# Moving the split, the store and the next load of a converted chunk within its eight steps

## The chip, the cores and the metric

The kernel runs on one core of one Trainium2 chip. The metric is the device time of one execution in microseconds (us). Three runs of the kernel before gave a median of 2088.47 us, from 2087.82 to 2095.43 us. In the listings PE is TensorE, DVE VectorE, ACT ScalarE, POOL GpSimd, and SP the engine that issues most of the DMAs, in order, one after another.

## The reference

Three parts follow one another. The first is attention with random features, and its output is reshaped to 2304 tokens of 512 values. The second is a mixture of eight experts in which every token goes through every expert. The third is one more pair of matrices, which are given in doubles (float64).

```python
x = np.ascontiguousarray(attn_out.transpose(0, 2, 1, 3)).reshape(B * S, H * D)
for e in range(E):                       # E = 8, w1[e]: 512 x 1024, w2[e]: 1024 x 512
    h = np.maximum(x @ w1[e], 0.0)
    ye = h @ w2[e]
    out += P[:, e:e + 1] * ye
h = x @ w_in                             # 512 x 2048, float64
g = h - np.tanh(h)
return (g @ w_out).astype(np.float32)    # 2048 x 512, float64
```

P is a gate that is normalized over rows and columns eight times.

## The kernel before

**Tiling.** The 2304 tokens are cut into three superblocks of 768 tokens. After the attention the program goes through the superblocks for the experts (kind 0, s = 0, 1, 2), then through the superblocks for the last pair of matrices (kind 1). In kind 0 a superblock is a loop over 32 groups Q (8 experts, 4 quarters of the hidden width each). Each float32 operand is held as a high and a low part (float32r), and a product is three matmuls: high by high, high by low, low by high. The first layer of a group in superblocks 1 and 2 is `quad7` (seven products of a Strassen scheme, in PSUM banks a, b and e, line 1259), and between its products stands the second layer, `group` (line 1434). A steady group holds 84 matmuls of 384 columns.

**Order.** The order on every engine is the order in which the program emits its instructions. Each engine works through its own queue in order and waits on semaphores. Between two products the program calls `between`, which among other things calls `tick` twice. So a group has 14 ticks. A tick advances the weight preparation `wprep` (in superblock 2: one load of a prepared unit `u`, line 296, and one of a prepared unit `y`, line 318, both on SP), the preparation of x, and in 26 of 32 ticks the background generator `bg`. Once every four groups `load_p` (line 1524) loads the gate values of the next expert, spread over all partitions, also on SP.

**The conversion.** In the third superblock the background generator is `convert(..., fine=True)`. It turns the last matrices' doubles into float32, one chunk of 128 x 256 doubles after another. One chunk takes eight steps of the generator. Its instructions are, on DVE: a clamp of the high words (line 1199), a shift (1203), a merge (1206), an exponent mask (1210), a product with the low words (1213); then an absolute value on ACT (1216) and an addition on POOL (1217); then a last product on DVE (1222), which gives the chunk `x` in float32. Of the 64 chunks, 27 are converted in the first superblock and 37 in the third: 32 whose result is split at once, and 5 "plain" ones whose float32 result is stored as it is (line 1226).

**The split chunks.** For these, `split_up` makes the high part (`V.tensor_copy`, line 1179) and the low part (`low`, line 1172), both written over the raw tile `r` from which the doubles were read. `put` (line 1176) stores `r` to DRAM, in one DMA or two, 48 in all, and `ld` (line 1186) loads the doubles of a later chunk. There are three raw tiles `r`: three loads are made ahead, and the load of chunk n+3 goes into the tile of chunk n. So SP holds that load until the store of chunk n has left the tile. The list `after` holds what is still to be done for the chunk just converted; `step()` takes one entry from it at each of the generator's yields, so its first entry is taken in the first step of the next chunk. Before the change the list of a split chunk has eight entries: nothing, nothing, high part, nothing, low part, nothing, store, load. For a plain chunk it is the load alone.

Of the kernel before, what the change touches and what calls it, by code (L numbers as in the profile page):

```python
# [20 lines left out]
def performer_moe_kernel(ctx, tc, q, k, v, omega, wg, w1, w2, win64, wout64, out):  # L21
# [1135 lines left out]
    def convert(raws, work, fine):  # L1157
        V = nc.vector
        bits = lambda w: struct.unpack("f", struct.pack("I", w))[0]
        big, small = bits(0x47EFFFFF), bits(0x38100000)  # L1160
        after = []

        def step():
            f = after.pop(0) if after else None
            if f:
                f()

        def split_up(x, r, dst, key):
            both = r.rearrange("p n t -> p (n t)").rearrange("p (h n) -> p h n", h=2).bitcast(F32R)

            def low():
                V.tensor_tensor(both[:, 1], x, both[:, 0].bitcast(F32), ALU.subtract)

            def put():
                for to, src in dst(both.bitcast(F32)):
                    nc.sync.dma_start(to, src)
                left[key] -= 1

            return [None, None, lambda: V.tensor_copy(both[:, 0], x), None, low, None, put]

        def ld():
            if not cjobs or halt[0]:
                return None
            key, src, dst = cjobs.pop(0)
            r = raws(f"r64_{len(cjobs)}")
            nc.sync.dma_start(r, src.bitcast(U32).rearrange("p (n t) -> p n t", t=2))
            return r, dst, key

        nx = [ld(), ld(), ld()] if fine else [ld()]
        for _ in range(16 if fine else 1):  # L1190
            yield
        while nx[0]:
            r, dst, key = nx.pop(0)
            if not fine:
                nx.append(ld())
            lo, hi = r[:, :, 0], r[:, :, 1]
            c, t, h, x = work(f"cw{converted[0]}")
            cf, xf = c.bitcast(F32), x.bitcast(F32)
            V.tensor_scalar(cf, hi.bitcast(F32), big, -big, ALU.min, ALU.max)
            if fine:  # L1200
                yield
                step()
            V.tensor_scalar(t, c, 3, 0x3FFFFFFF, ALU.logical_shift_left, ALU.bitwise_and)
            yield
            step()
            V.scalar_tensor_tensor(h, c, 0xC0000000, t, ALU.bitwise_and, ALU.bitwise_or)
            if fine:
                yield
                step()
            V.tensor_scalar(t, h, 0xFF800000, None, ALU.bitwise_and)  # L1210
            yield
            step()
            V.scalar_tensor_tensor(xf, lo, 2.0**-52, t.bitcast(F32), ALU.mult, ALU.mult)
            yield
            step()
            nc.scalar.activation(cf, cf, AF.Abs)
            nc.gpsimd.tensor_tensor(xf, xf, h.bitcast(F32), ALU.add)
            yield
            step()
            yield  # L1220
            step()
            V.scalar_tensor_tensor(xf, cf, small, xf, ALU.is_ge, ALU.mult)
            if callable(dst):
                after.extend(split_up(xf, r, dst, key))
            else:
                nc.sync.dma_start(dst, xf)
                left[key] -= 1
            if fine:
                after.append(lambda: nx.append(ld()))
            converted[0] += 1  # L1230
            yield
            step()
        while after:
            step()
            yield
# [459 lines left out]
    for st in stages:  # L1695
        kind, s = st
        if kind == 0 and s == 0:
            for Q in range(NQ):
# [4 lines left out]
                if Q == 2 * NQE + 3:  # L1703
                    phase.close()
                    pace[1] = 3
                    cv = phase.enter_context(tc.tile_pool(name="cvp", bufs=1))
                    bg.append(
                        convert(
                            lambda n: cv.tile([P, CW, 2], U32, tag="r64", name=n, bufs=2),
                            lambda n: [  # L1710
                                cv.tile([P, CW], U32, tag=f"c{i}", name=f"{n}{i}", bufs=1 + i // 3) for i in range(4)
                            ],
                            False,
                        )
                    )
                    next(bg[0])
# [26 lines left out]
        elif kind == 0:  # L1743
            for Q in range(NQ):
# [6 lines left out]
                if s == 2 and Q == 1:  # L1751
                    halt[0] = False
                    cjobs[:] = later_jobs + cjobs
                    pace[4] = 26
                    bg.append(
                        convert(
                            lambda n: rawp.tile([P, CW, 2], U32, tag="rs", name=n, bufs=3),
                            lambda n: [
                                x[:, i] for x in [sump.tile([P, 4, CW], U32, tag="s", name=n)] for i in range(3)
                            ] + [cxp[0].tile([P, CW], U32, tag="x", name=f"{n}x")],  # L1760
                            True,
                        )
                    )
# [103 lines left out]
```

## Time and profile before

| | |
|---|---|
| median of 3 runs | 2088.47 us |
| the profiled execution's own time | 2088.66 us |
| its span (first to last instruction) | 2086.9 us |
| PE busy | 2021.9 us (97%) |
| DVE busy | 1574.3 us (75%) |
| ACT, POOL busy | 1395.7, 1410.0 us |
| DMA, mean over the span | 241 GB/s |

The span is counted from the first instruction; between its end and the own time lie 1.8 us. In a listing of windows each row is one stretch: its ends and its length in us, then for each engine the busy time and the number of instructions, then TensorE's granted clock as a share of full speed, the busy share of the DMA engines, and GB/s. In a listing of waits the three numbers are the sum in us, the number of times, and the longest. In a listing of one line the durations are in ns (least, median, greatest), followed by the first and the last start in us. In a timeline a row is the start, the duration, engine, line, operation, output<-input, count, and in brackets how long the engine had been idle and what ended that.

### The profile page before, as it was taken

Reading aid. Unit: us, or ns where it says so; the run is one execution under the profiler, and the core shown is the slowest. Engines: PE = TensorE matmul, PEld = TensorE weight load, DVE = VectorE, ACT = ScalarE, POOL = GpSimd, SP = SyncE. Lnnn points to the kernel's source line nnn. Section 1 sums busy time; section 2 is a strip of 40 time slices with the busy share of each in tenths; the row PEclk is TensorE's granted clock in tenths of the full one; section 3 lists DMA queues with packets and bytes.
Section 4 is the critical chain, followed back from the end, with each engine's and each line's share of the span. In section 5 each row is a group of like instructions: output and inputs, shape, how many; then the busy total and the mean of one; then the engine's idle time right before and its main releaser. Section 6 shows DMA issues by size and latency. Waiting matters only on the chain.

```text
span 2086.9 us, 37530 instructions
## 1 busy us (share of the span) xinstructions
PE 2021.9 (97%) x11408; PEld 1885.1 (90%) x11408; DVE 1574.3 (75%) x3056; ACT 1395.7 (67%) x3426; POOL 1410.0 (68%) x1783
## 2 busy tenths in 40 slices
PE   9999999999999999999999999899999999999999
PEld 7777989899998999999999998888999988999998
DVE  8885867989886565766656677577876489999897
ACT  7884343344443577778777687677777778777775
POOL 7876877878874588888888666566666555254352
PEclk9999999999999999999999999999999999999999
DMA  6545977897876688999988877787888661441410
GB/s 171 137 134 181 369 276 261 288 336 269 282 265 230 211 312 289 330 344 357 320 299 310 326 270 271 269 312 255 263 296 306 232 217 54 139 152 65 168 46 31
DMA packets 357081, 503.24 MB, mean 241 GB/s; under 512 B 72448, under 2 KB 169616, under 8 KB 356880
## 3 DMA queue, kind: packets, MB, share of 16 engines
q1 hardware_dynamic: 350736, 493.44, 69.2%
q10 hardware_dynamic: 6144, 7.40, 1.1%
q8 instruction: 92, 1.51, 0.3%
q14 instruction: 109, 0.89, 0.1%
HBM read 351.75 MB, written 148.97 MB: 240 GB/s over the span
## 4 chain that ended last, share of the span: by engine, by line
PE 69%; DMA 10%; DVE 9%; POOL 5%; issue 3%; ACT 2%; SPq 1%; ACTq 0%; DVEq 0%; POOLq 0%
PE l L1575 20%; PE Y L1434 13%; PE b L1259 11%; PE p L1535 8%; PE e L1259 7%; PE a L1259 7%; DMA st<-r 3%; PE X L1434 2%; DMA u<-st 2%; POOL tmp L633 2%; DMA y<-st 1%; POOL eq L793 1%; DMA r<-in_moe_w_out_dram 1%; DMA r<-in_moe_w_in_dram 1%; DMA st<-y 1%
## 5 line engine op out<-in xcount | busy, mean ns | idle before, releaser
L1434 PE MATMUL Y<-h,y 128*128 128x384 f32 x2394 | 491.5, 338 | 14.1 <-ACT Y L1426 13.6
L1575 PE MATMUL l<-v,h 128*128 128x512 f32 x2016 | 482.6, 392 | 5.3 <-ACT x L113 1.8
L1575 PEld LDWEIGHTS l<-v,h 128*128 128x128 f32 x2016 | 375.4, 188 | 83.2 <-ACT h L1563 3.5
L1434 PEld LDWEIGHTS Y<-h,y 128*128 128x128 f32 x2394 | 424.0, 190 | 22.3 <-ACT Y L1426 21.2
L1259 PE MATMUL b<-x,u 128*128 128x384 f32 x1728 | 351.4, 338 | 20.4 <-DVE t L1358 13.4
L1343 POOL TENSOR_TENSOR h<-t,h 128x384 fp32r<-128x384 f32 x223 | 230.4, 1033 | 192.6 <-ACT h L1340 166.9
L1450 ACT COPY seven<-Y 128x384 f32<-128x384 f32 x534 | 247.4, 481 | 145.0 <-PE Y L1434 142.0
L1259 PEld LDWEIGHTS b<-x,u 128*128 128x128 f32 x1728 | 306.2, 189 | 28.3 <-DVE t L1358 15.1
L1426 ACT COPY Y<-seven 128x384 f32<-128x384 f32 x558 | 262.8, 488 | 4.0 <-DVE seven L1448 4.0
L1343 POOL TENSOR_TENSOR h<-h,h 128x384 fp32r<-128x384 f32 x192 | 202.7, 1060 | 51.6 <-ACT h L1340 43.2
L1259 PE MATMUL a<-x,u 128*128 128x384 f32 x1152 | 231.8, 335 | 1.8 <-POOL u L116 1.3
L1259 PE MATMUL e<-x,u 128*128 128x384 f32 x1152 | 232.3, 336 | 0.0
L1564 POOL TENSOR_TENSOR h<-t,h 128x384 fp32r<-128x384 f32 x94 | 95.9, 1020 | 187.9 <-ACT h L1563 185.7
L1535 PE MATMUL p<-x,u 128*128 128x384 f32 x1152 | 210.1, 337 | 2.3 <-DMA u<-st 1.6
L1535 PEld LDWEIGHTS p<-x,u 128*128 128x128 f32 x1152 | 202.6, 188 | 6.7 <-DMA u<-st 2.2
L1259 PEld LDWEIGHTS a<-x,u 128*128 128x128 f32 x1152 | 202.7, 188 | 3.5 <-POOL u L116 1.7
L1259 PEld LDWEIGHTS e<-x,u 128*128 128x128 f32 x1152 | 203.8, 189 | 0.0
L116 POOL TENSOR_TENSOR v<-rs,v 128x256 fp32r<-128x256 f32 x152 | 121.3, 827 | 53.6 <-ACT v L113 41.1
L1340 ACT CAST h<-t 128x384 fp32r<-128x384 f32 x224 | 115.7, 517 | 50.7 <-DVE t L1336 28.6
L1610 DVE SCALAR_TENSOR_TENSOR acc<-l,pt,acc 128x512 f32<-128x512 f32 x144 | 104.8, 744 | 27.8 <-PE l L1575 26.1
L113 ACT CAST u<-s 128x256 fp32r<-128x256 f32 x128 | 49.4, 409 | 105.9 <-POOL u L116 42.2
L116 POOL TENSOR_TENSOR u<-s,u 128x256 fp32r<-128x256 f32 x128 | 97.4, 778 | 22.5 <-ACT u L113 21.8
(410 smaller groups left out, 3711.8 us busy)
## 6 DMA issues: line engine op xcount, KB each, us to landing
u<-st SPq DMA_DIRECT2D x496, 256.0 KB, 5.2
y<-st SPq DMA_DIRECT2D x336, 256.0 KB, 5.0
st<-u SPq DMA_DIRECT2D x224, 256.0 KB, 3.8
rs<-in_moe_w_dram SPq DMA_DIRECT2D x128, 256.0 KB, 4.7
st<-y SPq DMA_DIRECT2D x128, 256.0 KB, 5.7
st<-v SPq DMA_DIRECT2D x96, 256.0 KB, 5.2
rq<-in_moe_w_dram SPq DMA_DIRECT2D x32, 512.0 KB, 4.8
v<-st SPq DMA_DIRECT2D x24, 512.0 KB, 6.0
```

What stands on the lines that cost most here:

```text
L113: nc.scalar.copy(dst[:, 0], src)
L116: eng.tensor_tensor(dst[:, 1, i : i + w], src[:, i : i + w], dst[:, 0, i : i + w].bitcast(F32), ALU.subtract)
L1259: nc.tensor.matmul(ps[:, :TB], u[:, wi, c], x[:, xi, c], start=(start and m == 0), stop=(stop and m == 5), skip_group_check=True,)
L1340: nc.scalar.copy(H[k][:, 0], src)
L1343: eng.tensor_tensor(H[k][:, 1], src, H[k][:, 0].bitcast(F32), ALU.subtract)
L1426: nc.scalar.copy(cell[0], xacc[i][:, d])
L1434: nc.tensor.matmul(ps, uw[i, g][0][:, wi, d * P : (d + 1) * P], Hs[g][i][:, hi], start=(n == 0 and not cell), stop=(n == 3 * len(gs) - 1), ...
L1450: nc.scalar.copy(xacc[i][:, d], ps)
L1535: nc.tensor.matmul(ps, u1[f + i][:, wi, c], ux[state["x0"] + 2 * t + i][:, xi, c], start=(m == 0), stop=(m == 11))
L1564: nc.gpsimd.tensor_tensor(lo, s, hi.bitcast(F32), ALU.subtract)
L1575: nc.tensor.matmul(ps, hh[f][0][:, hi, t : t + P], u2[n + f][:, wi], start=(f == 0 and i == 0), stop=(f == len(hh) - 1 and i == 2),)
L1610: V.scalar_tensor_tensor(a, ps, p[:, e : e + 1], a, ALU.mult, ALU.add)
```

## The change

A split chunk's list becomes: high part, low part, nothing, store, nothing, nothing, nothing, load. So the high part is made in the first step behind the conversion, the low part in the second, the store is issued in the fourth, and the load stays in the eighth. For a plain chunk in the third superblock seven empty entries are put ahead of its load, so that it too comes in the eighth step.

```diff
@@ in split_up
-            return [None, None, lambda: V.tensor_copy(both[:, 0], x), None, low, None, put]
+            return [lambda: V.tensor_copy(both[:, 0], x), low, None, put, None, None, None]
@@ behind a chunk's conversion
             else:
                 nc.sync.dma_start(dst, xf)
                 left[key] -= 1
+                after.extend([None] * 7 if fine else [])
             if fine:
                 after.append(lambda: nx.append(ld()))
```

## Rows read from the trace of the kernel before

**Rows 1.** Windows: superblock 1 (30 groups), then superblock 2 (29 groups).
```profile
709.80:1149.28 439.48, 437.79 (x2522) 436.64 (x2521) 279.04 (x490) 342.52 (x844) 367.92 (x420) 1.00 0.91 317
1181.03:1647.41 466.38, 436.74 (x2437) 428.13 (x2437) 323.20 (x607) 350.02 (x847) 298.30 (x299) 0.98 0.81 277
```

**Rows 2.** Windows: two of seven long groups, a steady one, sum of eight.
```profile
1256.32:1274.91 18.59, 16.41 (x85) 16.09 (x85) 13.73 (x26) 12.94 (x33) 10.14 (x11) 0.91 0.82 288
1306.34:1329.66 23.32, 17.31 (x85) 16.67 (x85) 11.41 (x25) 12.58 (x30) 11.39 (x12) 0.85 0.78 279
...
1409.64:1424.20 14.56, 14.56 (x86) 14.56 (x85) 11.23 (x25) 11.27 (x29) 10.10 (x12) 1.00 0.84 284
sum 150.35, PE 126.77 PEld 122.94 DVE 95.13 ACT 96.59 POOL 84.76; mean PE 15.85 PEld 15.37 DVE 11.89 ACT 12.07 POOL 10.59
```

**Rows 3.** Waits of PE, DVE and SP in 1181.03:1647.41.
```profile
PE b L1259 <- DVE t L1358: 13.4, 5, 5.3
...
DVE cw L1199 <- DMA r<-in_moe_w_out_dram: 39.6, 11, 10.1
...
DVE cw L1199 <- DMA r<-in_moe_w_in_dram: 21.8, 9, 5.8
...
SPq L1186 <- DMA st<-r: 125.3, 32, 6.4
SPq L318 <- PE Y L1434: 35.5, 29, 6.5
```

**Rows 4.** Timeline 1308:1324: one late load and whom it holds.
```profile
1312.18 0.59 SPq L1176 DMA_DIRECT2D st<-r  x1
...
1318.39 0.34 SPq L1186 DMA_DIRECT2D r<-in_moe_w_out_dram  x1
...
1321.51 0.29 DVE L1199 TENSOR_SCALAR cw<-r 128x256 f32<-128x256 f32 x1 [10.14 <-DMA r<-in_moe_w_out_dram]
...
1323.19 1.33 PE L1259 MATMUL b<-x,u 128*128 128x384 f32 x3 [5.27 <-DVE t L1358]
```

**Rows 5.** Line 1176, the store of the split parts, in superblock 2.
```profile
L1176 SPq DMA_DIRECT2D st<-r x48: 370/525/1328, 1209.2 to 1574.2; - x48
...
DMA to landing us min/median/max: 4.3/5.5/7.5
```

**Rows 6.** Landing times of line 1186 (doubles), then of line 1524 (gate), superblock 2.
```profile
DMA to landing us min/median/max: 2.5/3.1/6.6
...
DMA to landing us min/median/max: 8.6/9.1/9.8
```

**Rows 7.** Lines 296 and 318 (loads of units), then 1199 (clamp), superblock 2.
```profile
L296 SPq DMA_DIRECT2D u<-st x202: 319/430/2703, 1180.4 to 1640.1; - x101
...
L318 SPq DMA_DIRECT2D y<-st x202: 319/385/1287, 1181.4 to 1647.1; - x101
...
L1199 DVE TENSOR_SCALAR cw<-r x37: 281/487/1109, 1191.2 to 1603.3; 128x256 f32<-128x256 f32 x37
```

**Rows 8.** Timelines: gate load beside its group's first product, superblock 1, then 2.
```profile
753.48 1.20 PE L1259 MATMUL a<-x,u 128*128 128x384 f32 x6
753.52 0.43 SPq L1524 DMA_DIRECT2D pb<-pd  x1
...
1290.62 1.20 PE L1259 MATMUL a<-x,u 128*128 128x384 f32 x6
...
1299.54 0.49 SPq L1524 DMA_DIRECT2D pb<-pd  x1
```

**Rows 9.** Lines 1179 (high part) and 1172 (low part): a short and a long.
```profile
L1179 DVE CAST r<-cw35x x1: 285/285/285, 1293.5 to 1293.5; 128x256 fp32r<-128x256 f32 x1
...
L1179 DVE CAST r<-cw40x x1: 1110/1110/1110, 1358.6 to 1358.6; 128x256 fp32r<-128x256 f32 x1
...
L1172 DVE TENSOR_TENSOR r<-cw34x,r x1: 1234/1234/1234, 1285.9 to 1285.9; 128x256 fp32r<-128x256 f32 x1
L1172 DVE TENSOR_TENSOR r<-cw35x,r x1: 416/416/416, 1295.2 to 1295.2; 128x256 fp32r<-128x256 f32 x1
```

## The prediction

> **What bounds the kernel now.** I read the windows first, one group of the loop at a time. TensorE sets the end nearly everywhere: in superblock 1 the 30 groups take 439.48 us [rows 1], and a steady group takes 14.56 us [rows 2], so 30 x 14.56 = 436.8 and only 2.7 us are lost. Superblock 2, the one that converts, takes 466.38 us for 29 groups [rows 1], and 29 x 14.56 = 422.2: 44.1 us are lost there. The reader should see that the number of matmuls per group is the same and only the time differs. The loss is not even: seven groups and a steady one take 150.35 us together [rows 2], so the seven take 135.8 where 7 x 14.56 = 101.9 would do, 33.9 of the 44.1. The other 22 groups lose 10.2, or 0.47 each. In the longest groups the granted clock is below 1 as well (0.85 and 0.91 [rows 2]): TensorE ran partly at 1.2 in place of 2.4 GHz behind its own pauses, which is part of the loss and goes with them.
>
> Then the waits, engine by engine, backwards. The greatest wait of TensorE is for a DVE addition of the group's scheme (13.4 us in 5 [rows 3]). The greatest waits of DVE are those of the clamp, which opens a chunk, for its doubles: 39.6 + 21.8 = 61.4 us in 20 [rows 3]. The greatest of SP, by far, is that of the doubles' load for the store of the split parts out of the same raw tile: 125.3 us in 32, 3.9 each [rows 3]. One place shows the chain whole [rows 4]: the store is issued at 1312.18, the load only at 1318.39, the clamp starts at 1321.51 after 10.14 us of idle DVE, and TensorE, which needs the DVE instructions queued behind the clamp, has then idled for 5.27 us.
>
> The doubles should not be late: their load is emitted nine steps ahead of the clamp that reads them. It is SP that is behind. The gate load, which SP gets to in the same order, starts 0.04 us after its group's first product in superblock 1 and 8.92 us after it in superblock 2 [rows 8].
>
> **The change part by part.** Steps first. A chunk takes 8 steps; with 26 of 32 ticks and 14 ticks in 14.56 us a step is 1.28 us where nothing is lost (a chunk 10.24 us). Measured with the losses: 37 clamps from 1191.2 to 1603.3 [rows 7], 11.4 us a chunk, 1.43 a step.
>
> *Store from the seventh step to the fourth.* The store lands 5.5 us after its issue (4.3 to 7.5 [rows 5]). Before, the load follows one step later: 5.5 - 1.4 = 4.1 us of stall, against 3.9 measured. After, four steps lie between, 4 x 1.28 = 5.1 us: a stall of 0.4 at the median and 2.4 at the longest landing. Over 32 chunks this is 13 to 77 us in place of 125.3; I take 15, since the median is what repeats.
>
> When SP is behind, the steps' time doesn't count, only what it has to issue. A chunk's 9.85 ticks hold as many unit loads, of 0.41 us each (median 0.430 and 0.385 [rows 7]): 4.0 us. Its 1.5 stores of 0.53 [rows 5] add 0.8, its load 0.34 [rows 4]: 5.2 us. Before, 1.2 unit loads (0.5 us) lie between store and load, the stall is 5.5 - 0.5 = 5.0, the sum 10.2 of 10.24 us: once SP is late, it stays late, and every gate load, which lands 3.6 us later than a store (9.1 against 5.5 [rows 5, 6]), throws it back further. After, 4.9 unit loads (2.0 us) lie between, the stall is 3.5, the sum 8.7: SP makes up 1.5 us with each chunk, of which the gate loads, one in four groups or 5.7 chunks, take 0.6. So it catches up, slowly.
>
> What that gives the doubles: from the load's place to its clamp are 9 x 1.28 = 11.5 us; landing takes 3.1 (at most 6.6 [rows 6]), so SP may be 8.4 us late (4.9 in the bad case). It is 8.92 late now. Without the 3.5 us a chunk of avoided stall it stays inside that.
>
> *The loss that goes.* I charge the seven long groups to the late doubles. From one side: the seven fall to what the other 22 lose, 29 x 0.47 = 13.6 remain, 30.5 are gained. From the other: the 22 also owe half of theirs to late doubles, 5 more, 35.6. DVE's additional instructions stay, and with them the small collisions. I take 33.5, between the two.
>
> *High and low part two and three steps earlier.* Same instructions, no new wait: both read what DVE itself has written, and the raw tile's doubles are already used up. The store stays two steps behind the low part. Queued behind them on DVE are the next chunk's clamp and shift and the group's additions. A high part takes 0.29 or 1.11 us, a low part 0.42 or 1.23 [rows 9]; if all of them were long where all are short now, DVE has 32 x (0.82 + 0.81) = 52 us more; if the reverse, as much less. I take nothing, since both places lie between instructions of the same kind, and keep the bound for a rival.
>
> *Plain chunks.* Five of them; two further loads of doubles move seven steps back and then have the slack of every other chunk, 11.5 us. The seven empty steps at the end, 9 us, lie in the superblock's last groups, past the last clamp at 1603.3 [rows 7], while the superblock goes on beyond 1647 [rows 1]. Nothing waits for them: 0, and if the cover were gone, still no instruction in them.
>
> *What is late next.* SP's waits for TensorE to give up unit tiles (35.5 us in 29 [rows 3]) are SP being ahead, and grow. DVE's collisions stay and are in the 10 to 13.6 us.
>
> Sum, against the profiled execution's own 2088.66 us (span 2086.9 and 1.8 around it; the median of the runs is 2088.47, 0.2 less): 2088.7 - 33.5 = 2055.2, so 2055.
>
> **Two rules of the Trainium skill beside it.** The store's landing is 5.5 us for 256 KB [rows 5]. The Trainium skill, "DMA: Bandwidth & Descriptors", section "Anatomy of one DMA — SWDGE (gpsimd) path", gives about 2.0 us plus bytes over 436 GB/s, an estimate of 2.6 us by that page (its path is GpSimd's). By it SP's sum before would be 5.2 + 2.1 = 7.3 of 10.24 us, SP would not be behind at all and the change would be worth nothing; the trace disagrees, with 3.9 us of stall.
>
> High parts come in two lengths, 0.29 and 1.11 us [rows 9]. The Trainium skill, "SBUF — State Buffer", section "Who interferes with whom", has a DVE copy and a GpSimd instruction shut each other out of a shared port pair, whoever issues first. By it the first step is a poor place for the copy, since GpSimd has just been busy for the same chunk; the two lengths agree with the rule, and what it could cost is the third rival.
>
> **The rivals.** *Half of it.* SP stays behind for long stretches, since gate loads and waits for unit tiles throw it back faster than 0.9 us a chunk makes up; the stall then is 3.5 in place of 3.9 or 5.0, and about half of the late doubles stay. For it: at least one of the longest groups, 1306.34, comes straight after a gate load [rows 2, 8]. Against it: superblock 1 has the same gate loads and no lag [rows 8]. Time: 2088.7 - 17 = 2072.
>
> *Nothing.* The doubles are late for the gate loads alone and the store's wait is only where SP happens to stand. Against it: 125.3 us of SP's 466 in that wait. Time 2088.
>
> *Slower: the crowd at the chunk's end.* The last product, the high part, the clamp, the low part and the shift now come one behind the other on DVE, and the group's additions queue behind them. DVE's lost time costs TensorE at 44.1 / 61.4 = 0.72. To use up 33.5 us DVE must lose 46.6, or 1.46 us a chunk, of the 1.63 that high and low part could lose [rows 9]; the clamp (0.28 to 1.11 [rows 7]) adds up to 0.83. At 2.2 us a chunk: 2088.7 - 33.5 + 32 x 2.2 x 0.72 = 2106. Against it: the ticks hold the same number of instructions as before on average.
>
> **How the numbers follow.** Forecast 0.72, own range 2047 (the small losses mostly gone, 42 gained) to 2064 (25 gained); half 0.18, 2064 to 2078; nothing 0.05; slower 0.05. The range of 2046 to 2072 leaves out the last two, half of the second and little else. About 0.5% (10 us) is what a measurement of this kernel tells from no change: faster 0.90 (the first two), same 0.05, slower 0.05.
>
> **What would show it.** Right: SP's wait of the doubles' load for the store falls from 125 to below 40 us; the clamp's waits from 61.4 to below 10; the gate load starts within 3 us of its group's first product; the long groups come down to 14.6 to 15.5; superblock 2 to about 433 us, nothing changes outside it. Wrong: the clamp's waits stay above 30 us, or they go and TensorE waits as long for DVE additions behind longer copies.

## The result, and the profile after

The changed kernel takes 2065.33 us (median of 6 runs, 2062.83 to 2069.72) against 2090.59 for the kernel before (6 runs, 2087.65 to 2096.33). The ratio is 0.9877, 95% interval 0.9857 to 0.9897: faster by 1.2%. The prediction was faster, 2055, with a range of 2046 to 2072. The result lies in that range, but above the 2047 to 2064 that the forecast gave to its own mechanism. The profiled execution took 2062.83 us, 25.8 less than that of before.

The windows of superblocks 1 and 2 after (columns as before; line numbers below the edit are one higher in this kernel) answer to [rows 1]:

```profile
711.06:1150.40 439.34, 437.12 (x2519) 435.97 (x2517) 278.44 (x489) 342.16 (x843) 367.37 (x419) 1.00 0.90 316
1182.12:1623.78 441.66, 428.05 (x2438) 421.58 (x2438) 325.52 (x607) 348.73 (x847) 297.53 (x299) 1.00 0.87 293
```

The 25 us are all in superblock 2: 466.38 became 441.66 us for the same 29 groups and the same matmuls, so the loss against 29 x 14.56 fell from 44.1 to 19.4. Superblock 1 is unchanged. The granted clock of superblock 2 went from 0.98 to 1.00: the long pauses, and the time at the lower of the two clocks behind them, are gone together.

The windows of the groups that were longest before (three of the seven, and the sum of all seven and a steady one) answer to [rows 2]:

```profile
1257.70:1272.94 15.24, 14.84 (x85) 14.52 (x85) 12.46 (x25) 12.66 (x33) 10.17 (x10) 1.00 0.95 333
1302.64:1318.83 16.19, 14.86 (x85) 14.54 (x85) 12.20 (x24) 11.59 (x29) 10.11 (x12) 1.00 1.01 372
1334.61:1351.58 16.97, 14.83 (x85) 14.51 (x85) 13.60 (x29) 11.57 (x29) 10.20 (x12) 1.00 0.91 321
...
sum 124.35, PE 117.98 PEld 116.25 DVE 99.35 ACT 92.93 POOL 82.26; mean PE 14.75 PEld 14.53 DVE 12.42 ACT 11.62 POOL 10.28
```

The seven lost 33.9 us and now lose 124.35 - 14.56 - 101.92 = 7.9, that is 1.1 each. The other 22 lost 10.2 and now lose 11.5. So most of what the long groups lost is gone (the longest now takes 16.97 us), but a loss of about 0.7 us per group is left where the prediction had 0.3 to 0.47.

The waits in superblock 2 after, of SP, DVE and TensorE, answer to [rows 3]:

```profile
SPq L1186 <- DMA st<-r: 59.3, 22, 6.5
SPq L318 <- PE Y L1435: 52.4, 39, 6.5
...
DVE cw L1199 <- DMA r<-in_moe_w_out_dram: 10.1, 3, 4.2
...
PE Y L1435 <- ACT Y L1427: 12.0, 14, 2.1
```

SP's wait for the store went from 125.3 to 59.3 us, the clamp's waits for doubles from 61.4 us in 20 to 10.1 in 3, and TensorE's waits for a DVE addition (13.4 us) have left the list. What TensorE waits for now is ACT's copy of an accumulator into PSUM (line 1427). This wait is not new. It was TensorE's second greatest in superblock 2 before, and of the same size:

```profile
PE Y L1434 <- ACT Y L1426: 10.5, 14, 2.2
```

The gate load beside its group's first product (timeline), which answers to the second pair of [rows 8]:

```profile
1287.50 1.20 PE L1260 MATMUL a<-x,u 128*128 128x384 f32 x6
1291.57 0.43 SPq L1525 DMA_DIRECT2D pb<-pd  x1
```

SP stands 4.07 us behind at this gate load instead of 8.92.

One of the 13 pauses of TensorE above 0.3 us that are left, in the timeline of POOL, DVE, ACT and PE. All 13 end 3.7 to 5.4 us into a group, and 12 of them end with ACT's copy. The group of this one begins at 1504.64:

```profile
1503.91 2.17 POOL L1344 TENSOR_TENSOR h<-h,h 128x384 fp32r<-128x384 f32 x2
...
1503.99 1.22 DVE L1222 SCALAR_TENSOR_TENSOR cw55x<-cw,cw55x 128x256 f32<-128x256 f32 x1
...
1505.25 0.99 DVE L1179 CAST r<-cw55x 128x256 fp32r<-128x256 f32 x1
...
1506.16 0.28 DVE L1199 TENSOR_SCALAR cw<-r 128x256 f32<-128x256 f32 x1
1506.36 0.55 DVE L1375 TENSOR_TENSOR e<-e,t 128x384 f32<-128x384 f32 x1
...
1506.94 0.56 DVE L1337 SCALAR_TENSOR_TENSOR t<-e,pb 128x384 f32<-128x384 f32 x1
...
1507.54 0.51 ACT L1341 CAST h<-t 128x384 fp32r<-128x384 f32 x1 [1.86 <-DVE t L1337]
...
1507.95 0.47 ACT L1351 COPY t<-a 128x384 f32<-128x384 f32 x1
...
1508.33 0.49 ACT L1427 COPY Y<-seven 128x384 f32<-128x384 f32 x1
...
1508.86 0.98 PE L1435 MATMUL Y<-h,y 128*128 128x384 f32 x4 [0.94 <-ACT Y L1427]
```

Read it from below. TensorE idles 0.94 us for ACT's copy of line 1427. That copy stands on ACT behind another copy (1351) and a high part (1341), which waited 1.86 us for DVE's last sum of the previous group (1375, 1337). That sum stood on DVE behind the last product of a chunk (1.22 us), its high part (0.99) and the next chunk's clamp. The changed kernel can put a chunk's high part into just this place. In three of the 12 pauses a high part starts within 4 us ahead of the last sum; in the others clamps, low parts, shifts, merges or masks stand there. This crowd is what the later experiments go after.

### The profile page after: what moved, and what is told of

It reads as the page before. It is cut to its first block, busy times and chain, and to the rows that moved or that the text cites. A ratio compares the mean times of both kernels' runs of the same rounds, so it can differ in the third digit from the quotient of the medians.

```text
span 2061.0 us, 37514 instructions
## 1 busy us (share of the span) xinstructions
PE 2011.0 (98%) x11408; PEld 1876.4 (91%) x11408; DVE 1578.3 (77%) x3056; ACT 1395.9 (68%) x3426; POOL 1410.5 (68%) x1783
## 4 chain that ended last, share of the span: by engine, by line
PE 75%; DVE 8%; DMA 6%; POOL 5%; issue 3%; ACT 3%; SPq 1%; ACTq 0%; DVEq 0%; POOLq 0%
PE l L1576 21%; PE Y L1435 15%; PE b L1260 12%; PE e L1260 8%; PE p L1536 8%; PE a L1260 8%; PE X L1435 2%; POOL tmp L633 1%; DMA u<-st 1%; DMA st<-r 1%; DMA xd<-seven 1%; POOL eq L793 1%; DMA y<-st 1%; POOL h L1344 1%; DVE r L1179 0%
## 5 line engine op out<-in xcount | busy, mean ns | idle before, releaser
L1435 PE MATMUL Y<-h,y 128*128 128x384 f32 x2394 | 486.6, 335 | 16.2 <-ACT Y L1427 15.5
L1435 PEld LDWEIGHTS Y<-h,y 128*128 128x128 f32 x2394 | 419.6, 188 | 24.2 <-ACT Y L1427 23.3
L1359 DVE TENSOR_TENSOR t<-b,t 128x384 f32<-128x384 f32 x64 | 35.6, 556 | 105.6 <-PE b L1260 105.6
```

The source lines that it names most:

```text
L1435: nc.tensor.matmul(ps, uw[i, g][0][:, wi, d * P : (d + 1) * P], Hs[g][i][:, hi], start=(n == 0 and not cell), stop=(n == 3 * len(gs) - 1), ...
```

## The experiments

The theory: store and load stood one step apart, so SP lost about 4 us per chunk, fell behind, and the doubles came late to a DVE whose queue TensorE needs. The first rival: the gain is the earlier parts. The others: gate loads hold SP back; DVE is crowded at the chunk's end.

**The parts alone early.** Store and load stay in the seventh and eighth step.

```diff
-            return [None, None, lambda: V.tensor_copy(both[:, 0], x), None, low, None, put]
+            return [lambda: V.tensor_copy(both[:, 0], x), low, None, None, None, None, put]
```

> The kernel before with the high part in the first step and the low part in the second, as in the changed kernel, but the store left in the seventh step and the load in the eighth. Theory (the store is too close ahead of the load, SP falls behind, the doubles come late): the wait of the doubles' load for the store stays near 125 us, the clamp's waits near 60 us, time 2085 to 2095. Rival (the gain comes from DVE making the parts earlier): 2063 to 2070. Rival (crowding of DVE at the chunk's end costs something): above 2095.

Measured: 2092.01 us (10 runs), ratio 0.9986 (0.9966 to 1.0006). SP waits and the clamp waits as before:

```profile
SPq L1186 <- DMA st<-r: 128.0, 32, 6.4
...
DVE cw L1199 <- DMA r<-in_moe_w_out_dram: 46.3, 13, 13.5
DVE cw L1199 <- DMA r<-in_moe_w_in_dram: 11.2, 5, 3.7
```

Making the parts early is worth nothing by itself; the first rival falls.

**The load alone later.** Parts and store in their old steps, the load in the eleventh, that is in the third step of the next chunk.

```diff
             if fine:
-                after.append(lambda: nx.append(ld()))
+                if not callable(dst):
+                    after.extend([None] * 7)
+                after.append(None)
+                if converted[0] > 27:
+                    i, f = len(after) - 6, after[-6]
...
+                    after[i] = both_of
```

The function left out, `both_of`, does what stood in that entry (the third) and then makes the load.

> The kernel before with the parts in the third and fifth step and the store in the seventh, as before, but the load moved back from the eighth step to the eleventh (the third of the next chunk), so that four steps lie between store and load as in the changed kernel. Plain chunks load in the eleventh too. Theory (distance of store and load): the load's wait for the store falls from 125 to 40 to 70 us, the clamp's waits to below 20 us, time 2058 to 2070, although the doubles are asked for later than before. Rival (parts made earlier): 2085 to 2095. Rival (doubles are late because they are asked for late): above 2090.

Measured: 2073.18 us, ratio 0.9903 (0.9873 to 0.9934). The waits in its superblock 2:

```profile
SPq L1186 <- DMA st<-r: 44.5, 21, 4.7
...
DVE cw L1199 <- DMA r<-in_moe_w_out_dram: 14.2, 5, 6.1
DVE cw L1199 <- DMA r<-in_moe_w_in_dram: 10.8, 4, 3.6
```

Loads that are asked for three steps later arrive in better time. The size missed the expectation a little (25.0 us of the clamp's waits against 20, 2073 against 2070); three steps less slack may be the reason, which no run shows.

**A fourth raw tile.** This takes away what the load waits for, with every step as before.

```diff
...
+    def raw4(n):
+        rawn[0] += 1
+        pool, bufs = (r4p[0], 1) if rawn[0] % 4 == 0 else (rawp, 3)
+        return pool.tile([P, CW, 2], U32, tag="rs", name=n, bufs=bufs)
...
-                            lambda n: rawp.tile([P, CW, 2], U32, tag="rs", name=n, bufs=3),
+                            raw4,
```

> The kernel before, every instruction in its old step, with a fourth raw tile, so that a load goes into a tile whose store was issued nine steps earlier. Theory: the load's wait for the store all but goes (below 10 us), the clamp's waits fall below 15 us, time 2055 to 2066. Rival (gate loads and waits for unit tiles hold SP back, not the store): the clamp's waits stay above 30 us, 2075 to 2090. Rival (parts made earlier): 2085 to 2095.

Measured: 2061.06 us (4 runs), ratio 0.9844 (0.9815 to 0.9874). The window and the waits of its superblock 2 (line 1191 is its load, 1204 its clamp):

```profile
1184.15:1620.34 436.19, 427.19 (x2437) 421.67 (x2437) 318.66 (x607) 348.21 (x847) 297.06 (x299) 1.00 0.86 295
...
SPq L1191 <- DMA st<-r: 1.5, 2, 1.0
...
DVE cw L1204 <- DMA r<-in_moe_w_out_dram: 7.1, 2, 3.8
DVE cw L1204 <- DMA r<-in_moe_w_in_dram: 2.4, 2, 1.7
...
PE Y L1439 <- ACT Y L1431: 9.0, 14, 1.2
```

With its wait gone the clamp's waits are 9.5 us. The store's wait is the cause of the late doubles, shown by its removal. The gate loads as the cause fall: they are all still there.

**The same in the changed kernel.** The fourth raw tile added to it.

> The changed kernel with a fourth raw tile: parts in the first two steps, store in the fourth, load in the eighth. Theory (the changed kernel's remaining 59 us of SP waiting for the store cost it little): SP's wait goes, the clamp's 10 us of waits fall to 5 to 9, time 2059 to 2064. Beside the fourth tile with the old steps (2061 there) it shows what making the parts early is worth by itself: nothing by the theory, 2 to 4 us slower by the theory of crowding in the first step.

Measured: 2065.41 us, ratio 0.9875 (0.9855 to 0.9896). SP's wait for the store left its list of waits, the clamp's waits fell to 6.4 us, and the time is that of the changed kernel. So the 59 us that SP still waits there cost nothing.

```profile
1183.09:1625.59 442.50, 429.56 (x2437) 423.10 (x2437) 324.78 (x607) 348.40 (x847) 297.65 (x299) 1.00 0.85 292
...
PE Y L1440 <- ACT Y L1432: 12.5, 14, 2.2
```

With the fourth tile the old steps take 2061.06 and the new ones 2065.41, the ratios 0.9844 and 0.9875: the new steps cost about 4 us (superblock 2 loses 13.9 with the old steps and 20.3 with the new, and TensorE's waits for ACT's copy are 9.0 and 12.5). The intervals of the two ratios overlap, so the losses of the two traces carry this more than the medians. I charge it to the parts, which moved on DVE; the store moved too, and no run with the fourth tile parts the two. The expectation had this size for the theory of crowding; the first theory, which had nothing here, is wrong on this point.

**The addition on DVE.** The chunk's last product waits for POOL's addition for 22.7 us in all in superblock 2 after.

```diff
-            nc.gpsimd.tensor_tensor(xf, xf, h.bitcast(F32), ALU.add)
+            (V if fine else nc.gpsimd).tensor_tensor(xf, xf, h.bitcast(F32), ALU.add)
```

> The changed kernel with the addition of a chunk (line 1217) on DVE in place of POOL in the third superblock. It asks where the 19 us come from that superblock 2 still loses. Theory P (DVE stands waiting for POOL's addition in front of the last product, 20 us in all): those waits go, time 2052 to 2061. Theory C (DVE's own instructions crowd in front of the group's additions): 37 more DVE instructions of about 0.4 to 0.5 us, time 2065 to 2072.

Measured: 2062.71 us, ratio 0.9853 (0.9823 to 0.9882): between the two theories. The loss in superblock 2 is 19.4 us as in the changed kernel, though these waits have gone (5.0 us of waits for ACT are left in front of the last product).

> The kernel before with a fourth raw tile and the chunk's addition on DVE, all steps as before. If DVE's 24 us of waiting for POOL in front of the last product cost TensorE anything by themselves, this is 3 to 8 us faster than the fourth raw tile alone (2053 to 2058); if they are idle time that nobody misses, 2059 to 2064.

Measured, with the fourth tile and the old steps: 2058.48 us, ratio 0.984 (0.9819 to 0.986). This too falls between the two expectations, and its interval overlaps that of the fourth tile alone. Neither settles it.

**A quiet place.** In superblock 2 the conversion takes no step in the two ticks between the sixth and the seventh product, and one in each of the other twelve.

```diff
-                    pace[4] = 26
+                    pace[4] = 32
...
                 def between(k):
                     slot(7 * g + k)
+                    pace[2] = s == 2 and k == 5
```

> The changed kernel, but in the third superblock the conversion takes no step in the two ticks between a group's sixth and seventh product (between(5)), and one in each of the other twelve (12 steps a group in place of 11.4 on average). It asks about what superblock 2 still loses: all of TensorE's pauses above 0.3 us lie 3.7 to 5.4 us into a group, where the second layer waits for ACT's copy, which stands behind a high part of the group's last sum, which DVE makes behind the conversion's instructions. Theory (these instructions crowd in front of the last sum): the pauses at this place go from 13 to 4 or fewer, 19.4 us of loss fall to 6 to 12, time 2052 to 2059. Rival (DVE has too much work in superblock 2 wherever it stands): pauses appear at other places, 2063 to 2072.

Measured: 2049.65 us (4 runs, 2049.08 to 2050.12), ratio 0.9798 (0.9774 to 0.9822), the fastest kernel here. Its superblock 2, and all the waits of TensorE in it that the list shows:

```profile
1182.20:1610.58 428.38, 425.54 (x2438) 423.55 (x2438) 316.94 (x607) 348.44 (x847) 296.38 (x299) 1.00 0.88 302
```

```profile
PE b L1260 <- DVE t L1359: 2.0, 1, 2.0
PE X L1435 <- ACT seven L1451: 0.4, 1, 0.4
PE Y L1435 <- ACT Y L1427: 0.3, 1, 0.3
```

TensorE's waits for ACT's copy fell from 12.0 us in 14 to 0.3 in one, and 6.1 of the 19.4 us of loss remain. DVE still has the same 607 instructions in the stretch: it was not their number that counted, but where they stand. Whether that is the place or the regular 12 steps, the next run tells.

**The control.** The two quiet ticks between the third and fourth product (`k == 2`) instead.

> The control to the quiet place of 2050: the changed kernel with the same 12 steps a group, but the two ticks without a step lie between the third and fourth product. Theory (it is the place in front of the last sum that counts): the pauses 3.7 to 5.4 us into a group stay, 2062 to 2070. Rival (12 steps a group, three chunks in two groups, are what helps, wherever the gap lies): 2048 to 2055.

Measured: 2061.87 us, ratio 0.9848 (0.983 to 0.9866), with the pauses where they were:

```profile
1183.87:1621.60 437.73, 426.67 (x2438) 421.79 (x2438) 297.50 (x607) 347.28 (x847) 297.23 (x299) 1.00 0.86 295
...
PE Y L1435 <- ACT Y L1427: 10.4, 14, 1.6
```

With the same 12 steps a group, the place is worth 12 us by the medians and 9.4 by the losses in superblock 2 (15.5 here, 6.1 with the quiet place). DVE is even less busy here (297.50 us against 316.94), so its amount of work is not what costs. 2061.87 is just under what the theory had; the regular 12 steps may be worth some 3 to 4 us of their own (a loss of 15.5 against 19.4), though the interval overlaps that of the changed kernel.

**Both causes gone with the old steps.** Fourth raw tile and quiet place.

> The kernel before with a fourth raw tile, parts, store and load in their old steps, and no step of the conversion between the sixth and seventh product. Theory: both causes gone at once, superblock 2 loses 4 to 9 us, time 2049 to 2056. Rival (the two are the same loss, or the denser steps elsewhere bring the late doubles back): 2058 to 2066.

Measured: 2050.64 us, ratio 0.9803 (0.9783 to 0.9823). As expected, and equal to the changed kernel with the quiet place: once the crowd is gone, it makes no difference whether the store is moved or a tile is added.

**The quiet place in the kernel before.**

> The kernel before, store and load in the seventh and eighth step, with no step of the conversion between the sixth and seventh product. If late doubles and the crowd in front of the last sum are two causes that add, the late doubles stay (SP's wait for the store 120 us or more, the clamp's waits 40 to 65) and 8 to 15 us go: 2075 to 2084. If the quiet place alone were enough: 2050 to 2060. If a denser conversion makes the doubles later still: 2088 to 2100.

Measured: 2118.68 us, ratio 1.0119 (1.0096 to 1.0142), slower by 1.2%, further than even the third expectation. The waits in its superblock 2:

```profile
SPq L1186 <- DMA st<-r: 149.2, 30, 6.6
...
DVE cw L1199 <- DMA r<-in_moe_w_out_dram: 78.4, 18, 13.3
DVE cw L1199 <- DMA r<-in_moe_w_in_dram: 42.8, 10, 8.5
```

This is the prediction's account of SP at work. With 12 steps a group a chunk takes 8/12 x 14.56 = 9.7 us, while the old order, with 9.3 unit loads in place of 9.85, costs SP 10.0: it falls back with every chunk, and the clamp waits 121 us. Its waits for the store are 149.2 us in 30, or 5.0 each, as the prediction's sum has them for an SP that is behind. The changed order costs 8.5 by the same sum and keeps up (with the quiet place the clamp waits 12.7 us). So the same edit gains 16 us behind the change and loses about 25 without it.

**Quiet place and the addition on DVE.**

> The changed kernel with the quiet place and the chunk's addition on DVE. The quiet place alone left 1.2 us of waits in front of the last product, so by the theory that these waits were a sign of the crowd and not a cause, nothing is gained: 2048 to 2053, or up to 4 us slower for 37 more DVE instructions. If the addition's round trip to POOL costs something by itself: 2044 to 2047.

Measured: 2054.31 us, ratio 0.9815 (0.9797 to 0.9832), 4.7 us above the quiet place alone and a little beyond the expectation's "up to 4 us slower". The waits for POOL in front of the last product were a sign of the crowd; taking them away with more DVE work gains nothing and rather loses (superblock 2 loses 9.4 us, against 6.1).

**The plain chunks' edit undone.**

> The changed kernel without the seven empty entries ahead of a plain chunk's load: the plain chunks ask for the next doubles in the first step again, as in the kernel before. The prediction put this edit at nothing: 2062 to 2069. If loads asked for early are worth something in the last five chunks (4.2 us of the clamp's waits lie there): 2059 to 2062; if two loads that crowd behind one another hold up SP: 2069 to 2074.

Measured: 2066.43 us, ratio 0.9875 (0.985 to 0.99): nothing, as predicted.

## Why the prediction was right, and where its size was off

*The chain.* Store, load, clamp, TensorE: confirmed at each link. The late doubles went with the distance (load later: 25 us of clamp waits left, changed kernel: 10.1) and with the wait itself (fourth tile: 9.5).

*SP's account.* It held where it mattered: which kernel keeps up and which falls back. One unit load a tick, as its sum has it, is the trace's average: 202 of line 296 and 202 of line 318 [rows 7] in 29 x 14 = 406 ticks. The stall left was mis-sized: 59.3 us, within the 13 to 77 stated but not the 15 taken. SP is behind in part of the chunks and then has only the unit loads between store and load. It didn't matter, as the fourth tile in the changed kernel shows. For the same reason two of the signs named were missed (SP's wait below 40 us, the gate load within 3 us: 4.07 here) though the step was right. The clamp's waits, 10.1 us, are at the edge of the sign (below 10). Two more signs were missed for the loss that stays: four of the seven groups take more than 15.5 us, and superblock 2 takes 441.66 us, not 433.

*The gain.* 33.5 us were taken, from 30.5 to 35.6; 25.8 were measured between the profiles. In superblock 2 the sum leaves 44.1 - 33.5 = 10.6 us of loss, and 19.4 were measured. One term that failed is "high and low part two and three steps earlier: I take nothing". The new steps cost 4 us by the medians and 6 by the losses (fourth tile with old and with new steps). The two places were not alike: the group's last sum queues behind the chunk's end, and the high part now stands there at times. In the trace it does so in three of 12 pauses; how much of the 4 us is its own stays open. The third rival named this crowd and its place; it came to between an eighth and a fifth of what it needed to decide the sign.

*The loss that stays.* "The seven fall to what the other 22 lose" was the other term set too low: the seven lose 1.1 us each, since a group rid of late doubles still meets the crowd. Even with the old steps and no wait for the store (fourth tile) 13.9 us are lost, not 10.6. I took the greatest wait of TensorE and left out the second, 10.5 us for ACT's copy, and held the small losses for DVE's amount of work and as fixed. The quiet place took 13 of the 19.4 us, of which the control has about 4 for the regular steps and 9 for the place.

*How near it was.* 2065.33 lies in the range only by the part of it that belongs to the rival "half of it" (2064 to 2078). That the sign and the path were right is shown by the waits and the experiments; that the number fell inside the range owes something to luck.

*The rules.* The Trainium skill, "SBUF — State Buffer", section "Who interferes with whom", has a DVE copy wait for a GpSimd instruction that holds the shared ports. In the timeline above a high part of 0.99 us ends just behind POOL's subtraction, where a short one takes 0.29 [rows 9]; the trace agrees. All high parts of superblock 2 together take about 20 us in place of 16, all low parts 15 in place of 18, so the parts' own time is far from the 52 us of the prediction's bound. The crowd cost something, but no run here parts the ports' share from the queue's. The 2.6 us estimated from the Trainium skill, "DMA: Bandwidth & Descriptors", section "Anatomy of one DMA — SWDGE (gpsimd) path", would have made the change worthless; the stall and the fourth tile decide for the measured 5.5.

*Rivals.* "Half of it" (2072) and "nothing" (2088) fall with the clamp's waits, 10.1 of 61.4 us left.

## What to carry to other kernels

Where a load reuses a buffer that a store must first leave, the engine that issues both pays the store's landing time less what it has to issue in between, and everything queued behind pays with it: count its issue time and stalls per period against the period, since beyond it the lag no longer heals (10.0 us of work in a period of 9.7 made this kernel 1.2% slower). A wait that vanishes leaves the next queue as the limit; look for pauses at one fixed place of the loop before calling what is left noise. And the order of edits matters: an edit that gains 16 us behind a fix can lose 25 without it.

## What was not expected of the hardware

The landing time of a load of doubles rose from 3.1 us (median, [rows 6]) to 3.9 with SP less behind, while the DMA share in superblock 2 went from 0.81 to 0.87: the loads arrive sooner although each takes longer. With the fourth tile, where SP hardly waits for a store, the median is 5.1 us.

```profile
DMA to landing us min/median/max: 2.4/3.9/7.0
```
